# Gated linear attention and a feed-forward layer on one core: columns of the hidden layer renumbered, with another plan of loads and work

## The chip, the cores and the metric

The kernel runs on one core of one Trainium2 chip. The metric is the time of one execution on the device in microseconds (us): 185.11 us, the median of 3 runs (185.07 to 185.2).

## The reference

For each batch b (4) and head h (8), a state of 48 x 48 is carried over 768 steps; its output rows go through a feed-forward layer with 2048 hidden columns:

```python
f = 1.0 / (1.0 + np.exp(-f_logit))
for t in range(S):
    state = f[:, :, t, :, None] * state + np.einsum('bhd,bhe->bhde', k[:, :, t], v[:, :, t])
    y[:, :, t] = np.einsum('bhd,bhde->bhe', q[:, :, t], state)
x = y.transpose(0, 2, 1, 3).reshape(B * S, H * D)      # 3072 x 384
h = x @ w_in                                           # 384 -> 2048
return ((h * (1.0 / (1.0 + np.exp(-h)))) @ w_out)      # 2048 -> 384
```

Inputs and output are float32. The order of the 2048 hidden columns is free as long as w_in's columns and w_out's rows are taken in the same order.

## The kernel before

**Tiles.** The sequence is cut into chunks of 128 steps, 6 for each batch. Two chunks make one of 12 pairs. Pairs 0 to 3 (form T) hold chunks 0 and 1 of one batch, loaded together so that two neighbouring steps lie on one partition (runs of 384 bytes); pairs 4 to 11 (form N) hold the same chunk of two batches (runs of 192 bytes). Within a chunk the recurrence is done as matrices: cumulative sums of log f, their exponentials, q and k scaled by them, scores q k under a triangular mask, and the state carried from chunk to chunk.

**The plan.** Nothing is scheduled by a compiler. The string PLAN lists all work in order; a word is `kind.pair.part:engine:buffers`. Every engine takes its own words in the order in which they stand, and waits in that order (P TensorE, A ScalarE, V VectorE, G GpSimd with its DMA queue, S the DMA queue of SP). The numbers behind the second colon say which buffer of its class a result takes; `pb` are the eight PSUM banks. The kinds:

- `f k q v`: loads from HBM by SP (L225), 384 KB each or in halves. `wi`, `wo`: loads of quarters of w_in and w_out by GpSimd (L204, L207), float32 in HBM, bf16 in SBUF. These weights are loaded once and stay.
- `E`, `L`: exp and ln on ScalarE (L231, L235, L238), together log f. `cs`: cumulative sums on TensorE (L297 to L307). `a`, `ia`, `al`: their exponentials on ScalarE (L309, L311, L253).
- `ki`, `qg`: k and q scaled (L314). `vb`: v cast to bf16. `tq` and `qkc`: both transposed on TensorE (L321) and copied out of PSUM; `qkD` does that by a DMA of SP instead.
- `sc`: scores (L338, L342); `at`: mask (L346); `y`, `yi`: output rows (L260, L354, L358); `yc`: copy (L182 on ScalarE, L184 on VectorE, as all copies); `yT` and `xc`, or `yD`: transposed (L366, or by DMA L370). `d`, `sd`, `su`: the state's update (L272, L375, L379, L385).
- `mi.P.j`: hidden columns 256 j to 256 j + 255 of pair P, 6 matmuls (L246) with 256 columns of x as the moving operand; `mi.P.j.i` is its half for one chunk, 6 matmuls with 128. w_in is the stationary operand, 128 columns side by side for each matmul. `si`: SiLU on ScalarE (L251). `mo.P.i.g`: 4 of the 16 matmuls (L281) that give the output of chunk i of pair P, each for 128 hidden columns and 384 output columns. `oc`: copy out of PSUM, `so`: store (L289 for T, L291 for N).
- `idle.N.n::b`: n matmuls of zeros with N columns, filler for TensorE at the start (L426).

When ScalarE goes over from exponentials to SiLU or back, it loads a table (L477).

w_in is laid out in SBUF as 128 partitions x 3 x 2048 and w_out as 128 x 16 x 384. Hidden column n * 128 + p is column p of the n-th weight block, and row p of w_out's n-th block:

```python
w_in_src = moe_w_in.rearrange("(ko ki) n -> ki ko n", ki=128)
w_out_src = moe_w_out.rearrange("(ko ki) n -> ki ko n", ki=128)
```

A quarter of w_out, as `wo` loads it, therefore reads four separate rows of 1.5 KB for each partition.

Of the kernel before, what the change touches and what calls it, by code (L numbers as in the profile page):

```python
# [49 lines left out]
mi.0.1.0:P:1 vb.2.1:A:5 at.2.0.1:V: mi.0.1.1:P: si.1.2:A: mi.1.0.0:P: si.0.1:A: mi.1.1.1:P: d.2:P:5,7 si.1.0:A: si.1.1:A: y.2:P:0,2 sd.2.0:A:1  # L50
mi.0.5.0:P:1 yc.2.0:A:0 mi.1.4.0:P:3 su.2.0:G:0 mi.1.5.0:P:6 yT.2.0:P:5 mi.1.4.1:P: f.5.0:S:1 xc.2.0:V:2 su.1.1:G:0 mi.0.4.1:P:0 si.1.4:A: yi.2.1:P:
mi.0.4.0:P: yc.2.1:A:2 mi.0.7.1:P:5 wo.0:G: mi.1.5.1:P: yT.2.1:P:3 mi.0.7.0:P: xc.2.1:V: mi.0.5.1:P: sd.2.1:V:1 qg.3.0:G:1 mi.1.7.0:P:2 si.0.5:A:
k.4.0:S:4 mi.2.1:P:3 si.0.7:A: wo.1:G: mi.2.4:P:7 si.1.5:A: vb.3.1:V:6 mi.1.6.0:P:1 si.2.1:A:2 wo.2:G: ki.3.1:V:3 mi.1.7.1:P: ki.3.0:V: mi.2.0:P:5
wo.3:G: si.1.7:A: qg.3.1:V: mi.0.6.0:P:6 si.0.4:A: mi.0.6.1:P: tq.3.0:P:3 si.0.6:A: tq.3.1:P:2 qkc.3.0:V:1 si.2.0:A: mi.2.2:P:0 k.4.1:S: qkc.3.1:A:
mi.2.7:P:6 mi.2.6:P:5 si.2.7:A: cs.4.0:P:3 si.2.4:A: mi.1.6.1:P: vb.3.0:A:1 sc.3.0:P:2,6 si.2.6:A: mi.2.3:P:7 at.3.0.1:V:2 si.2.2:A: mo.1.1.0:P:5
at.3.0.0:V: si.1.6:A: d.3:P:6,0 si.2.3:A: mo.1.0.0:P:2 sd.3.0:V:0 sc.3.1:P:1,7 su.3.0:G:0 mo.1.0.1:P: at.3.1.1:V:3 k.5.1:S:5 al.4.1:A:4 mo.1.1.1:P:
su.2.1:G:0 sd.3.1:V:0 mi.2.5:P:6 at.3.1.0:V: mo.0.0.0:P:7 si.2.5:A: y.3:P:0,1 mo.2.0.0:P:6 mo.2.0.1:P: ia.4.0:A:3 yc.3.0:A:1 mo.0.0.1:P: E.5.0:A:1
f.6.0:S:2 mo.0.1.0:P:0 ia.4.1:A:1 ki.4.0:V:2 yi.3.1:P: mo.1.0.2:P: yc.3.1:A:0 a.4.0:A:2 mo.0.0.2:P: q.4.1:S:4 L.5.0:A:2 mo.1.1.2:P: a.4.1:A:4
mo.0.1.1:P: v.4.0:S:4 yT.3.0:P:1 mo.1.0.3:P: xc.3.0:V:3 q.5.1:S:5 ki.4.1:V:4 cs.5.1:P:4 mo.0.0.3:P: ia.5.1:A:0 v.4.1:S: al.4.0:A:5 oc.1.0:A:0
yT.3.1:P:1 mo.2.0.2:P: al.5.1:A:1 xc.3.1:V: qg.4.1:G: cs.5.0:P:3 q.5.0:S: mo.1.1.3:P: ia.5.0:A:3 E.6.0:A:0 mo.2.0.3:P: qkD.4.1:S:0 a.5.1:A:1  # L60
mi.3.5:P:2 oc.2.0:V:1 a.5.0:A:4 mi.3.4:P:1 qg.5.1:V:0 q.4.0:S: oc.1.1:V:2 mi.3.1:P:4 ki.5.1:V: vb.4.1:G:0 k.5.0:S: mo.0.1.2:P: si.3.5:A:3 vb.4.0:G:2
# [47 lines left out]
def kernel(  # L109
# [398 lines left out]
```

## Time and profile before

| | |
|---|---|
| median of 3 runs | 185.11 us |
| the profiled execution | 184.94 us |
| its span, first to last instruction | 183.2 us |
| TensorE busy | 173.3 us of the span |
| first matmul with w_in | at 24.2 us |
| first matmul with w_out | at 45.7 us |
| w_in issued | at 17.7, 21.6, 25.3 and 26.1 us |
| w_out issued | at 35.9, 37.7, 38.5 and 39.2 us |
| DMA | 31.91 MB in 109478 packets |

The page of the profile gives the busy time of each engine, its share in 40 equal slices, the chain of work that ended last, and the costliest groups of instructions by line. A matmul's time in a group runs from its start until its result is there, so matmuls that follow each other overlap; the rate at which they stream is read from the distance of their starts, or from a run of the same kind in the chain. Weight loads have a row of their own, PEld. DMA-issuing instructions of an engine do not count as busy; the time from issue to landing is told by the DMA view.

### The profile page before, as it was taken

The page shows a single profiled execution, that of the slowest core. Times are in us where ns is not written, and L with a number is a line of the kernel's source. Part 1 is how long each engine was busy: PE and PEld are TensorE (multiplying, and loading weights), DVE is VectorE, ACT ScalarE, POOL GpSimd, SP SyncE. Part 2 cuts the span into 40 slices and gives each one's busy share as a digit, 9 for nine tenths or more (in the row PEclk, how much of TensorE's full clock was granted, in tenths as well). Part 3 has the DMA queues.
Part 4 walks back from the last instruction along what each step waited for, and adds up shares of the span by engine and source line. Part 5 has one row for each costly group of instructions (what it writes and reads, how often), then busy time and mean ns, then how long its engine had stood idle before and what let it go on. Part 6 is the DMA issues. An engine that isn't in the chain of part 4 may idle for free.

```text
span 183.2 us, 4930 instructions
## 1 busy us (share of the span) xinstructions
PE 173.3 (95%) x2014; PEld 126.9 (69%) x2016; DVE 80.8 (44%) x169; ACT 136.1 (74%) x249; POOL 55.5 (30%) x99
## 2 busy tenths in 40 slices
PE   7988898999999999999999999999999999999990
PEld 2356687898666776678788667688766776888650
DVE  6068774052613529184554719340371854500030
ACT  4698997669994895879889995999697662287211
POOL 6043880570404000371055720271310440032010
PEclk9999999999999999999999999999999999999999
DMA  5999999999991997999996999468999997424115
GB/s 136 297 305 300 184 245 254 198 157 203 192 182 36 194 183 127 102 207 188 146 209 139 224 189 198 97 168 165 209 219 143 182 195 143 137 77 177 43 58 160
DMA packets 109478, 31.91 MB, mean 174 GB/s; under 512 B 103504, under 2 KB 109040, under 8 KB 109456
## 3 DMA queue, kind: packets, MB, share of 16 engines
q1 hardware_dynamic: 105136, 26.68, 73.3%
q0 software_dynamic: 4320, 4.92, 14.1%
q8 instruction: 16, 0.26, 0.6%
q14 instruction: 6, 0.05, 0.1%
HBM read 25.17 MB, written 4.72 MB: 163 GB/s over the span
## 4 chain that ended last, share of the span: by engine, by line
PE 76%; DMA 8%; ACT 7%; SPq 2%; DVE 1%; issue 1%; POOL 1%; DVEq 0%
PE pb L281 33%; PE pb L246 29%; DMA w_in_sb<-in_moe_w_in_dram 4%; PE pb L342 3%; DMA f<-in_f_logit_dram 2%; ACT x L309 2%; PE pb L354 2%; PE pb L358 2%; ACT lf L235 1%; DMA out_dram<-ob 1%; SPq L225 1%; PE pb L375 1%; PE pb L304 1%; PE pb L338 1%; POOL st L385 1%
## 5 line engine op out<-in xcount | busy, mean ns | idle before, releaser
L246 PE MATMUL pb<-xT,w_in_sb 128*128 128x256 bf16 (+1 forms) x672 | 69.8, 257 | 1.6 <-DMA w_in_sb<-in_moe_w_in_dram 1.3
L281 PE MATMUL pb<-w_out_sb,hT 128*128 128x384 bf16 x384 | 71.1, 326 | 0.0
L251 ACT ACTIVATE hT<-pb 128x512 bf16<-128x512 f32 x96 | 51.9, 608 | 20.0 <-PE pb L246 19.3
L246 PEld LDWEIGHTS <-w_in_sb 128*128 128x128 bf16 x672 | 57.1, 98 | 9.7 <-DMA w_in_sb<-in_moe_w_in_dram 1.8
L281 PEld LDWEIGHTS <-hT 128*128 128x128 bf16 x384 | 35.0, 97 | 19.6
L385 POOL TENSOR_TENSOR st<-sd,al 48x192 bf16<-48x192 f32 x40 | 20.8, 519 | 56.6 <-PE pb L354 24.1
L346 DVE TENSOR_TENSOR atm<-pb,triu 128x512 bf16<-128x512 f32 x32 | 20.7, 684 | 13.8 <-PE pb L342 12.7
L309 ACT ACTIVATE x<-pb 128x384 f32<-128x384 f32 x48 | 22.2, 512 | 5.9 <-PE pb L307 2.7
L477 ACT ACT_TABLE_LOAD x19 | 24.4, 1283 | 0.3
L184 DVE COPY ob<-pb 128x384 f32<-128x384 f32 x16 | 8.8, 553 | 22.2 <-PE pb L281 19.5
L314 POOL TENSOR_TENSOR qk<-q,x 128x384 bf16<-128x384 f32 x11 | 11.2, 1024 | 21.6 <-ACT x L309 8.4
L314 DVE TENSOR_TENSOR qk<-k,x 128x384 bf16<-128x384 f32 x18 | 10.9, 613 | 12.7 <-ACT x L309 12.7
L182 ACT CAST yb<-pb 128x384 bf16<-128x384 f32 x18 | 9.1, 506 | 7.6 <-PE pb L358 7.4
L379 DVE TENSOR_TENSOR sd<-pb,st 128x384 f32<-128x384 f32 x16 | 8.9, 553 | 11.4 <-PE pb L375 8.6
L291 POOL DMA_DIRECT2D out_dram<-ob x8 | 4.4, 559 | 30.7 <-DVE ob L184 17.0
L346 DVE TENSOR_TENSOR atm<-pb,mask 128x512 bf16<-128x512 f32 x16 | 10.6, 685 | 7.0 <-PE pb L338 6.9
L231 ACT ACTIVATE e<-f 128x768 f32<-128x768 f32 (+1 forms) x13 | 10.6, 812 | 2.8 <-DMA f<-in_f_logit_dram 2.8
L314 DVE TENSOR_TENSOR qk<-q,x 128x384 bf16<-128x384 f32 x13 | 7.2, 561 | 7.7 <-DMA q<-in_q_dram 7.1
L426 PE MATMUL pb<-zero,triu 128*128 128x512 bf16 (+1 forms) x26 | 8.9, 480 | 1.4 <-POOL triu masks.py:66 1.4
L184 DVE COPY xT<-pb 128x384 bf16<-128x384 bf16 x10 | 3.6, 357 | 14.4 <-PE pb L366 14.4
L314 POOL TENSOR_TENSOR qk<-k,x 128x384 bf16<-128x384 f32 x6 | 6.1, 1016 | 8.6 <-ACT x L309 7.5
L182 ACT COPY ob<-pb 128x384 f32<-128x384 f32 x8 | 3.9, 489 | 4.4 <-PE pb L281 4.4
(73 smaller groups left out, 150.3 us busy)
## 6 DMA issues: line engine op xcount, KB each, us to landing
f<-in_f_logit_dram SPq DMA_DIRECT2D x11, 384.0 KB, 5.3
k<-in_k_dram SPq DMA_DIRECT2D x16, 192.0 KB, 3.9
q<-in_q_dram SPq DMA_DIRECT2D x16, 192.0 KB, 3.9
v<-in_v_dram SPq DMA_DIRECT2D x16, 192.0 KB, 3.5
v<-in_v_dram SPq DMA_DIRECT2D x4, 384.0 KB, 7.0
q<-in_q_dram SPq DMA_DIRECT2D x4, 384.0 KB, 5.5
k<-in_k_dram SPq DMA_DIRECT2D x4, 384.0 KB, 5.7
w_in_sb<-in_moe_w_in_dram POOLq DMA_DIRECT2D x4, 384.0 KB, 7.7
```

The source lines that it names most:

```text
L182: nc.scalar.copy(dst, src)
L184: ENG[eng].tensor_copy(dst, src)
L231: return nc.scalar.activation(e, at("f", P)[:, j * w:(j + 1) * w], AF.Exp, scale=-1.0)
L246: nc.tensor.matmul(h[:, i, cols], w_in_sb[:, kk, n * 128:(n + 1) * 128], at("xT", P)[:, kk, cols], start=(kk == 0), stop=(kk == KT - 1))
L251: return nc.scalar.activation(at("hT", P)[:, 2 * j:2 * j + 2, :], at("h", P, j).rearrange("p (n c) -> p n c", n=2), AF.Silu)
L281: nc.tensor.matmul(o, at("hT", P)[:, n, i * C:(i + 1) * C], w_out_sb[:, n, :], start=(n == 0), stop=(n == NT - 1))
L309: nc.scalar.activation(at(kind, P, i).rearrange("p h d -> p (h d)"), at("cs", P, i)[:, 0:HD], AF.Exp, scale=1.0 if kind == "ia" else -1.0)
L314: ENG[eng].tensor_mul(at("qk", P, i)[:, j, :, 0:D], heads("qk"[j], P, i), at("ia" if j else "a", P, i))
L346: ENG[eng].tensor_mul(at("atm", P, i)[:, r], at(f"s{r}", P, i).rearrange("p (n c) -> p n c", c=C), mask[:, None, :].to_broadcast([C, NP, C]))
L379: nc.vector.tensor_add(at("sd", P, i), d_ps, prev_state(P, i))
L385: nc.gpsimd.tensor_mul(at("st", P, i)[lo:lo + D, :, r * D:(r + 1) * D], at("sd", P, i)[lo:lo + D, :, r * D:(r + 1) * D], al_of(P, i)[lo:lo ...
L477: nc.scalar.preload_act_table_set(turns[n])
```

## The change

1. *Hidden columns renumbered.* In a block of 512 hidden columns, partition ki now holds rows 4 ki to 4 ki + 3 of w_out, which lie side by side in HBM: 6 KB in one run for each partition of a quarter. To match, the j-th weight block of w_in takes every fourth column: the stationary operand of `mi` (L246) is now 128 columns with a step of 4 elements. w_in's loads stay as they are.
2. *Another plan.* All words stand in another order, and many copies and products are on another engine: `ki` 15 times on GpSimd and 9 on VectorE (before 6 and 18), `qg` 8 and 16 (11 and 13), `vb` 11 on GpSimd (6), `oc` 15 on ScalarE (8), `xc` 8 on ScalarE (2), `yc` 11 on VectorE (6). SP loads k and q ahead of v at the start and f.3 behind v.2. The words of w_in stand earlier on GpSimd, in the order 2, 1, 0, 3; the two `sc` of a chunk pair stand side by side; pairs 2 and 3 come in later. The fillers are 29 matmuls of 512 columns (before 26) and 4 of 128 (before 2). The transposes of q and k of 4.1 and 5.0 go from DMA to TensorE and that of 6.0 the other way: `tq` stands 11 times (before 10), `qkD` 13 times (before 14); `yT` with `xc` is done for 5.0 in place of 6.0. ScalarE changes its table 17 times within the plan (before 19).
3. *Last results in column halves.* `mo`, `oc` and `so` of pair 11 have a fourth or third number: columns 0 to 191 or 192 to 383 of the output. The 32 matmuls of 384 columns become 64 of 192.

The core of the diff, the start and the end of the plan and the code:

```diff
 PLAN = """
-f.0.0:S:0 f.0.1:S: f.1.0:S:1 v.0.0:S:0 q.0.0:S:0 E.0.0:A:0 E.0.1:A: L.0.0:A:0 k.0.0:S:0 E.1.0:A:1 f.2.0:S:2 L.0.1:A: idle.512.15::7 cs.0.0:P:0
-q.1.0:S:1 cs.0.1:P:1 a.0.0:A:0 L.1.0:A:1 qg.0.0:G:0 a.0.1:A:1 f.3.0:S:3 idle.512.3::7 cs.1.1:P:2 ia.0.0:A:2 ia.0.1:A:3 vb.0.1:G:0 cs.1.0:P:3 ki.0.0:V:
-a.1.0:A:4 k.1.0:S:1 qg.0.1:V:1 ia.1.0:A:0 idle.512.2::7 tq.0.0:P:4 a.1.1:A:2 ki.0.1:V: ia.1.1:A:1 vb.0.0:A:1 idle.512.1::7 tq.0.1:P:5 q.2.0:S:2
-E.2.0:A:0 d.0:P:6,7 qkc.0.1:V:0 L.2.0:A:2 qg.1.1:G:2 qkc.0.0:V: v.1.0:S:1 al.1:A:0 sd.0.0:V:0 idle.512.2::3 cs.2.1:P:0 qg.1.0:V:3 E.3.0:A:1
-sc.0.1:P:3,5 k.2.0:S:2 cs.2.0:P:2 at.0.1.1:V:0 sc.0.0:P:4,6 ia.2.0:A:3 a.2.0:A:2 ki.1.1:V: al.0:A:1 L.3.0:A:0 f.4.0:S:0 ki.1.0:V: su.0.0:G:0
-tq.1.1:P:5 at.0.0.1:V:1 a.2.1:A:4 tq.1.0:P:2 qkc.1.1:A:1 at.0.1.0:V: cs.3.1:P:1 wi.1:G: sd.0.1:V:1 cs.3.0:P:6 qkc.1.0:A: at.0.0.0:V: qg.2.0:G:4
-v.2.0:S:2 al.3:A:2 vb.1.0:A:2 idle.512.3::3 sc.1.0:P:3,5 ia.2.1:A:1 qg.2.1:G:0 y.0:P:7,4 vb.1.1:A:3 at.1.0.0:V:2 k.3.0:S:3 al.2:A:3 a.3.1:A:0
-yi.0.1:P: sc.1.1:P:2,0 ki.2.1:G: at.1.0.1:V: yc.0.0:A:0 ia.3.1:A:2 at.1.1.1:V:3 idle.128.2::3 d.1:P:3,7 yc.0.1:A:1 wi.0:G: ki.2.0:V: tq.2.1:P:5
-ia.3.0:A:4 sd.1.0:A:0 at.1.1.0:V: yT.0.1:P:1 yT.0.0:P:0 a.3.0:A:1 tq.2.0:P:4 su.1.0:G:0 qkc.2.1:V:0 xc.0.0:A:0 y.1:P:3,2 xc.0.1:A: q.3.0:S:3
-qkc.2.0:V: mi.0.2.0:P:6 su.0.1:G:0 yc.1.0:A:2 yi.1.1:P: mi.0.3.1:P:0 E.4.0:A:0 yc.1.1:V:1 sc.2.1:P:5,1 wi.2:G: yT.1.0:P:4 L.4.0:A:1 mi.0.3.0:P:
-...
-si.11.0:A:1 so.7.1:G: mi.11.3:P:6 si.11.1:A: so.4.0:G: mi.11.5:P:5 mi.11.4:P:1 si.11.5:A: mi.11.2:P:3 si.11.4:A: mi.10.3:P:5 si.11.2:A: mi.11.7:P:1
-si.10.3:A: mo.11.1.0:P:3 si.10.6:A: oc.9.0:A:0 mo.10.1.1:P: si.11.3:A: so.9.0:S: mo.11.0.0:P:5 si.11.7:A: mo.10.1.2:P: mo.10.1.3:P: mo.11.0.1:P:
-mo.11.0.2:P: mi.11.6:P:0 mo.11.1.1:P: si.11.6:A: mo.11.1.2:P: mo.11.1.3:P: mo.11.0.3:P: oc.11.1:V:1 mo.10.0.1:P: so.11.1:S: oc.11.0:V:5 mo.10.0.2:P:
-oc.10.1:V:4 so.1.1:S: so.11.0:G: so.10.1:S: mo.10.0.3:P: oc.10.0:A:3 so.10.0:S:
+f.0.0:S:0 f.0.1:S: f.1.0:S:1 k.0.0:S:0 q.0.0:S:0 E.0.0:A:0 E.0.1:A: L.0.1:A:0 f.2.0:S:2 L.0.0:A: idle.512.9::7 cs.0.1:P:0 E.1.0:A:1 cs.0.0:P:1
+q.1.0:S:1 L.1.0:A:1 ia.0.0:A:0 k.1.0:S:1 idle.512.4::7 cs.1.1:P:2 a.0.0:A:1 ki.0.0:V:0 a.0.1:A:2 cs.1.0:P:3 al.1:A:0 ia.0.1:A:3 a.1.1:A:4 v.0.0:S:0
+ki.0.1:G:1 qg.0.1:G: E.2.0:A:0 v.1.0:S:1 a.1.0:A:0 qg.0.0:G: ia.1.0:A:3 idle.512.12::7 tq.0.1:P:4 qg.1.0:V:2 L.2.0:A:2 k.2.0:S:2 wi.2:G: ia.1.1:A:2
+idle.512.1::7 tq.0.0:P:5 qkc.0.1:V:0 qg.1.1:G:3 cs.2.0:P:6 qkc.0.0:V: q.2.0:S:2 a.2.0:A:1 wi.1:G: ki.1.0:V: idle.512.3::3 sc.0.0:P:7,1 sc.0.1:P:3,2
+ki.1.1:G: vb.0.0:A:0 cs.2.1:P:4 at.0.1.0:V:0 vb.0.1:A:1 at.0.0.0:V:1 a.2.1:A:0 wi.0:G: idle.128.1::5 d.0:P:5,3 ia.2.1:A:4 at.0.0.1:V: v.2.0:S:2
+tq.1.0:P:7 al.0:A:1 sd.0.0:A:0 tq.1.1:P:0 at.0.1.1:V: su.0.0:G:0 qkc.1.0:A:1 qkc.1.1:V: idle.128.3::5 y.0:P:1,5 al.2:A:2 ia.2.0:A:3 wi.3:G: yi.0.1:P:
+yc.0.0:A:0 sc.1.1:P:2,7 yc.0.1:A:1 sc.1.0:P:4,0 at.1.1.1:V:2 vb.1.0:G:2 vb.1.1:A:3 yT.0.0:P:6 yT.0.1:P:1 xc.0.0:A:0 at.1.1.0:V: d.1:P:5,7 xc.0.1:A:
+at.1.0.1:V:3 mi.0.5.0:P:6 sd.1.0:A:1 mi.0.5.1:P: at.1.0.0:V: su.1.0:G:0 mi.0.4.0:P:2 mi.0.2.0:P:1 sd.0.1:V:0 y.1:P:5,0 su.0.1:G:0 yi.1.1:P: yc.1.0:A:2
+mi.0.2.1:P: yc.1.1:A:0 mi.0.3.0:P:4 yT.1.0:P:3 mi.0.3.1:P: f.3.0:S:3 xc.1.0:V:1 yT.1.1:P:5 mi.0.4.1:P: xc.1.1:V: mi.1.2.0:P:0 sd.1.1:V:1 si.0.5:A:0
+mi.1.3.0:P:3 mi.1.0.1:P:5 su.1.1:G:0 si.0.4:A: mi.1.5.1:P:7 si.0.2:A: mi.1.3.1:P: mi.1.1.0:P:6 wo.0:G: si.1.3:A:1 mi.1.4.0:P:2 mi.1.2.1:P: wo.1:G:
+mi.1.5.0:P: si.1.2:A: f.4.0:S:0 mi.1.1.1:P: wo.2:G: mi.0.7.1:P:1 si.1.5:A: mi.0.7.0:P: wo.3:G: si.1.1:A: mi.0.6.1:P:3 qg.2.0:V:4 si.0.7:A:
+...
+si.11.5:A: mo.11.0.0.0:P:3 si.11.7:A: mi.10.2:P:6 si.11.2:A: mi.10.5:P:2 si.11.6:A: si.11.3:A: mi.10.4:P:1 si.11.4:A: mo.11.1.0.0:P:7 si.10.2:A:
+mo.11.1.1.0:P: si.10.5:A: mo.11.1.2.0:P: mo.11.1.3.0:P: mo.11.0.1.0:P: oc.11.1.0:V:1 mo.11.1.0.1:P: so.11.1.0:G: mo.11.1.1.1:P: mo.11.0.2.0:P:
+so.8.1:G: mo.10.1.1:P: so.7.1:G: mo.11.0.3.0:P: so.9.0:G: mo.10.0.0:P:5 oc.11.0.0:A:2 si.10.4:A: so.11.0.0:S: mi.10.6:P:4 mo.10.0.1:P: si.10.6:A:
+mo.11.1.2.1:P: mo.10.0.2:P: mo.10.0.3:P: mo.11.1.3.1:P: oc.10.0:A:5 mo.10.1.2:P: oc.11.1.1:V: so.10.0:G: mo.11.0.0.1:P: so.11.1.1:G: mo.10.1.3:P:
+mo.11.0.1.1:P: oc.10.1:A:4 mo.11.0.2.1:P: mo.11.0.3.1:P: so.10.1:S: oc.11.0.1:A: so.11.0.1:S:
 """
...
@@ -158,7 +160,7 @@
     w_in_sb = sb.tile([128, KT, d_ff], BF16, name="w_in_sb")
     w_out_sb = sb.tile([128, NT, d_model], BF16, name="w_out_sb")
     w_in_src = moe_w_in.rearrange("(ko ki) n -> ki ko n", ki=128)
-    w_out_src = moe_w_out.rearrange("(ko ki) n -> ki ko n", ki=128)
+    w_out_src = moe_w_out.rearrange("(m ki j) n -> ki m j n", ki=128, j=4)
     SRC = {"f": f_logit, "k": k, "q": q, "v": v}
 
     plan = []
@@ -192,6 +194,10 @@
     def al_of(P, i):
         return at("al", P)[:, :, i] if PAIRS[P][0] == "T" else at("al", P, i)[:, :, 0]
 
+    def part_of(half):
+        w = d_model // 2
+        return slice(half[0] * w, (half[0] + 1) * w) if half else slice(0, d_model)
+
     def prev_state(P, i):
         b, c = PAIRS[P][1 + i]
         return at("st", *where_u[b, c - 1])
@@ -204,7 +210,7 @@
                 nc.gpsimd.dma_start(out=w_in_sb[:, :, n * w:(n + 1) * w], in_=w_in_src[:, :, n * w:(n + 1) * w])
             else:
                 w = NT // parts
-                nc.gpsimd.dma_start(out=w_out_sb[:, n * w:(n + 1) * w, :], in_=w_out_src[:, n * w:(n + 1) * w, :])
+                nc.gpsimd.dma_start(out=w_out_sb[:, n * w:(n + 1) * w, :].rearrange("p (m j) n -> p m j n", j=4), in_=w_out_src[:, n * w // 4:(n + 1) * w // 4])
             return
         P = rest[0]
         form, *us = PAIRS[P]
@@ -243,7 +249,7 @@
                 n = 2 * j + i
                 cols = slice(rest[2] * C, (rest[2] + 1) * C) if len(rest) > 2 else slice(0, 2 * C)
                 for kk in range(KT):
-                    nc.tensor.matmul(h[:, i, cols], w_in_sb[:, kk, n * 128:(n + 1) * 128], at("xT", P)[:, kk, cols],
+                    nc.tensor.matmul(h[:, i, cols], w_in_sb[:, kk, n // 4 * 512 + n % 4:(n // 4 + 1) * 512:4], at("xT", P)[:, kk, cols],
                                      start=(kk == 0), stop=(kk == KT - 1))
             return
         if kind == "si":
@@ -276,14 +282,16 @@
         b, c = us[i]
         last = c == CHUNKS - 1
         if kind == "mo":
-            o = at("o", P, i)[:, 0:d_model]
+            cols = part_of(rest[3:])
             for n in range(4 * rest[2], 4 * rest[2] + 4):
-                nc.tensor.matmul(o, at("hT", P)[:, n, i * C:(i + 1) * C], w_out_sb[:, n, :], start=(n == 0), stop=(n == NT - 1))
+                nc.tensor.matmul(at("o", P, i)[:, cols], at("hT", P)[:, n, i * C:(i + 1) * C], w_out_sb[:, n, cols], start=(n == 0), stop=(n == NT - 1))
         elif kind == "oc":
-            copy(eng, at("ob", P, i), at("o", P, i)[:, 0:d_model])
+            cols = part_of(rest[2:])
+            copy(eng, at("ob", P, i)[:, cols], at("o", P, i)[:, cols])
         elif kind == "so":
             r0 = b * S + c * C
-            ob, dst = at("ob", P, i), out[r0:r0 + C, :]
+            cols = part_of(rest[2:])
+            ob, dst = at("ob", P, i)[:, cols], out[r0:r0 + C, cols]
             if T:
                 for j in range(2):
                     ENG[eng].dma_start(out=dst.rearrange("(p j) n -> j p n", j=2)[j], in_=ob[j * HC:(j + 1) * HC])
```

## The prediction

> **What bounds the kernel now.** I read the page first (engines, slices, chain), then the chain in order of time, TensorE's waits, the timelines of ScalarE and GpSimd to 40 us, and the DMA landings.
>
> ```profile
> PE 173.3 (95%) x2014; PEld 126.9 (69%) x2016; DVE 80.8 (44%) x169; ACT 136.1 (74%) x249; POOL 55.5 (30%) x99
> ...
> PE   7988898999999999999999999999999999999990
> ...
> PEclk9999999999999999999999999999999999999999
> DMA  5999999999991997999996999468999997424115
> ```
>
> TensorE is full from the eighth slice to the last, at full clock; the DMA engines are full to 55 us (slice 12). The chain, in order of time:
>
> ```profile
> 6.25 0.84 ACT e L231
> ...
> 25.33 8.09 DMA w_in_sb<-in_moe_w_in_dram
> 33.47 1.18 PE pb L246 x18
> 34.65 0.17 PE pb L366 x3
> 34.82 0.67 PE pb L246 x12
> ...
> 63.48 3.27 PE pb L246 x30
> ...
> 174.18 4.56 PE pb L281 x28
> 178.77 0.48 ACT ob L182
> ```
>
> The start is a chain of attention steps and one transfer of w_in; from 33 us on nearly all is matmuls at the streaming rate: 3.27/30 = 109 ns with 256 columns, 4.56/28 = 163 with 384, 0.67/12 = 56 with 128. What TensorE waited for:
>
> ```profile
> PE pb L426 <- POOL triu masks.py:66: 1.4, 1, 1.4
> PE pb L246 <- DMA w_in_sb<-in_moe_w_in_dram: 1.3, 3, 0.7
> PE pb L297 <- ACT lf L235: 0.9, 2, 0.6
> ```
>
> So weights are what it waits for last before it is full. The sum therefore uses one quantity, the **lag**: the clock minus the useful matmul time issued so far (filler matmuls not counted). Per word of the plan I take 0.85 us for the cumulative sums of a T pair, 0.45 for `tq`, 0.35 for `sc` and `d`, 0.42 for a T `y`, 0.17 for `yi` and `yT`, and 0.34 for a half unit of `mi` (6 x 56 ns), all start to start in TensorE's timeline. Ahead of mi.0.7.1, the first that needs w_in's last quarter, these give 19.5 us; it ran when that quarter landed, at 35.9. Lag 16.4. At the end (159.0 us of matmul time, PE done at 178.6) it is 19.6: in 143 us only 3.2 were lost, of which single waits (0.5 at 101.0, 0.3 at 114.7, 0.2 at 110.5) make about 1.1. So time is won by a smaller lag when the weights are in, by less matmul work, or behind the last matmul; nowhere else.
>
> **The change, part by part.**
>
> *Loads and early plan.* When w_in is issued:
>
> ```profile
> 17.68 0.94 POOL L204 DMA_DIRECT2D w_in_sb<-in_moe_w_in_dram  x1
> 18.69 1.95 POOL L314 TENSOR_TENSOR qk<-q,x 128x384 bf16<-128x384 f32 x2
> 20.61 0.98 POOL L314 TENSOR_TENSOR qk<-k,x 128x384 bf16<-128x384 f32 x1
> 21.55 0.79 POOL L204 DMA_DIRECT2D w_in_sb<-in_moe_w_in_dram  x1
> 23.16 2.22 POOL L385 TENSOR_TENSOR st<-sd,al 48x192 bf16<-48x192 f32 x4 [0.83 <-DVE atm L346]
> 25.33 1.55 POOL L204 DMA_DIRECT2D w_in_sb<-in_moe_w_in_dram  x2
> ```
>
> The quarters landed at 24.1, 28.9, 33.4 and 35.9. After the change GpSimd has ki.0.1, qg.0.1 and qg.0.0 ahead of the first. Their start: the first three loads are the same, so E.1.0 begins at 6.25 again; E 0.78 and L 0.73 (start to start) give 7.75; ia.0.0, a.0.0, a.0.1 at 0.39, al.1 at 0.1, ia.0.1 at 0.39 give 9.4; three products at 0.96 give 12.4 (k0 and q0 come a place earlier in SP's queue: k0 where v0 landed, 7.4, and q0 at 8.7 as before). The first quarter (wi.2) is issued at 12.4 instead of 17.7. The next three follow behind qg.1.1, ki.1.1 and su.0.0: issues 14.3, 16.1, 17.9.
>
> Landings: the first quarter needed 6.5 us from issue, so 18.9. Those issued while another was in flight did not start until it had landed, and then came together: w_in's last two 4.5 and 2.5 us apart, w_out's last three 4.3, 2.6 and 2.7 apart. All three stand ready before 18.9, so 23.4 (wi.1), 25.9 (wi.0) and 28.5 (wi.3). SP's loads share the engines as before: in the packet records both queues get the same number of packets while both are full (about 192 each per us at 45 us), and SP's packets are smaller.
>
> Useful time ahead of the first user of each: mi.0.5.0 7.4, mi.0.2.0 8.4 (sums 2.54, `tq` 1.8, `sc` 1.4, `d` 0.7, `y` 0.42, `yi` 0.17, `yT` 0.34, `mi` 1.0), mi.1.0.1 11.7, mi.0.7.1 14.35. Lags: 23.4 - 8.4 = **15.0**, 25.9 - 11.7 = 14.2, 28.5 - 14.35 = 14.15. The attention chain is no later: tq.0.0 about 12.5, scores 14.0, four `at` of VectorE (0.61 each, from 14.7) 17.1, y.0 17.2, yc 17.8, `yT` and xc 19.8, thus mi.0.5.0 at 19.8, lag 12.5. w_out's first quarter is due at 15.0 + 19.6 = 34.6; GpSimd issues it behind su.1.1 at about 26.5, it starts when wi.3 has landed and with 4.3 to 5.6 us is there by 34.1. The lag becomes 15.0 instead of 16.4: **-1.4 us**. Bounds: 13 (quarters together at once) to 18.5 (rival 1).
>
> *Rows of w_out.* 512 runs of 6 KB are read instead of 2048 of 1.5 KB; bytes are equal. Written pieces are 768 B now, 83 ns each in the packet records, 170 us over 16 engines = 10.6. The nearest larger pieces are 1 KB (103 ns, w_in) and 3 KB (138 ns, stores): 512 of 3 KB cost between 4.4 and, at 4 x 83, 10.6 us. Either way it lies beside full matmuls: **0**; without this cover a quarter costs what it lands late, and the first has 0.5 us to spare (34.1 against 34.6). The Trainium skill (DMA: Bandwidth & Descriptors, Specifications) gives 512 B as the least size for line rate; by that 1.5 KB rows lose nothing already and the sum is the same, while the trace's 83 ns for 768 B against 103 ns for 1 KB show that size still matters a little.
>
> *Strided weights.* Every `mi` now loads 128 columns of w_in 4 elements apart. No row shows such a load. Lower end 0; no reason for a gain. Upper end: four times the stretch, four times the time: 224 ns instead of 56, 192 x 168 + 480 x (224 - 109) ns = 87 us. I take 0, since the nearest row, the contiguous load, keeps up with one every 56 ns and 480 of the 672 have 109 ns of streaming to hide in. The Trainium skill (SBUF — State Buffer, note on "SBUF cachelines") speaks of lines of 16 bytes and at least two hits on a line for full rate; 4 bf16 elements are 8 bytes, two hits, so by it the cost is nothing; no row here can show it.
>
> *Matmul work.* One `tq` more (8 x 56 = 0.45; `yT` only moves from pair 6 to pair 5) and pair 11's `mo` as 64 of 192 columns instead of 32 of 384: 64 x 82.5 - 32 x 162.5 = 0.08. **+0.5**.
>
> *Tail.* From the last matmul's end (178.7) to the span's end are 4.45 us: copy 0.48, SP issue 0.34, landing at 181.8, 1.35 to close. The copy of half the columns saves about 0.15 (0.48 with a fixed part; a 4-element one takes 0.19). The transfer is 96 KB instead of 192: pieces of 96 KB landed 2.1 and 2.4 us after issue where this took 2.55. **-0.35**; bounds 0 and -0.6. All other stores are issued earlier; mo.11.0's 12 half-column matmuls (1.0 us) cover oc.10.1 and its store.
>
> *The rest.* `ki`, `vb`, `oc`, `xc`, `yc` change engines: GpSimd gets 9 `ki` more at 1.0 us (30% busy), ScalarE two table loads fewer (1.28 each). Hidden while TensorE is full; without cover a product on GpSimd is 0.4 us later than on VectorE and stands ahead of SP's transposes. Later single waits: 1.1 us now, taken as the same; bounds 0 and 3 (rival 3).
>
> **Sum**: -1.4 + 0.5 - 0.35 = -1.25, from the profiled execution's 184.94 (span 183.2, 1.7 around it): 183.7; its own time is 0.17 below the median of 185.11, so for a median **183.9**.
>
> **Rivals.**
> 1. *The quarters come one by one*, 4.7 us apart, as the second did (24.1 to 28.9): 18.9, 23.6, 28.3, 33.0. mi.0.7.1 then has lag 33.0 - 14.35 = 18.6, since the new order does 5 us less attention work ahead of it: +2.2 + 0.5 - 0.35, **187.4, slower**. It decides from a landing of the last quarter after 30.8 on. For: the second quarter was alone because the third was issued too late. Against: all later ones came in groups. 0.15.
> 2. *Strided loads cost*, at twice the time (112 ns): 56 ns on the 174 half-unit matmuls from mi.0.2.0 on = 9.7, 3 ns on 480 = 1.4: **about 195**. The Trainium skill (Advanced Engine Details and Errata, SBUF Cachelines) tells of a penalty where every access meets another line. 0.1.
> 3. *New single waits eat the gain*: the order of 140 us is new, and one of 1 to 2 us at a transpose or a load brings **185**. For: SP's queue waits in order. Against: TensorE's waits sum to 1.1 now. 0.2.
> 4. *The weights are no bound at all*, lag 13: **182**. 0.05.
>
> Forecast 0.5. A measurement here tells 0.2% (0.37 us) from no change. Faster: forecast 0.47, rival 4, some of 3: 0.57. Same: 0.17, most of 3. Slower: 0.26 (rivals 1, 2, a share of 3). The range runs from 182.5 to rival 1's 187.4; it leaves out rival 2 and the ends.
>
> **What would show it.** First w_in issue near 12.4, landings 18.9, 23.4, 25.9, 28.5; a wait of about 2 us of L246 near 21; lag 15.0 at mi.0.7.1 (29.4 us); w_in's weight loads at 98 ns and `mi` at 109; end of PE to span end 4.1. Wrong: `mi` above 112 ns, a wait at 30 us, waits of over 1 us after 40.

## The result: slower, and the profile after

| | before | after |
|---|---|---|
| median of 4 runs | 185.16 us | 192.75 us |
| ratio to before, 95% interval | | 1.041 [1.0369, 1.0452] |
| profiled execution, its span | 184.94, 183.2 us | 192.34, 190.5 us |
| first matmul with w_in | 24.2 us | 25.7 us |
| lag at 35 us | 16.1 | 22.8 |
| TensorE done, to the span's end | 178.7, 4.45 us | 187.4, 3.08 us |

Medians are over all executions of a kernel; ratios leave out those that took over 1.5% more than its fastest.

The change costs 7.6 us where 1.2 of gain were forecast. The lag is counted as in the prediction. The page after, engines and slices:

```profile
PE 173.2 (91%) x2060; PEld 136.8 (72%) x2061; DVE 76.5 (40%) x155; ACT 134.1 (70%) x253; POOL 66.2 (35%) x115
...
PE   7889219999999999999979999998899998999993
...
PEclk9999855999999999999999999999999999999998
DMA  6999999999989900999359398795999599520133
```

TensorE's busy time is what it was. Two things are new: the hole in the fifth and sixth slice (19 to 28.6 us), and a granted clock that falls to half there and stays low for a slice after it. The last row, DMA, shows no such hole there: the transfers went on while TensorE stood.

What TensorE waited for, line by line: total, times, longest.

```profile
PE pb L252 <- DMA w_in_sb<-in_moe_w_in_dram: 6.5, 2, 4.1
PE pb L434 <- POOL triu masks.py:66: 1.4, 1, 1.4
PE pb L374 <- ACT yb L184: 1.2, 1, 1.2
PE pb L252 <- ACT xT L184: 1.1, 1, 1.1
PE pb L252 <- DVE sd L387: 1.1, 1, 1.1
```

Before, the matmuls with w_in waited 1.3 us for it, in three pieces; now 6.5 in two. TensorE's timeline (start, length, and in brackets the idle time before) shows where:

```profile
21.08 0.52 PE L278 MATMUL pb<-vb,qk 64*128 64x96 bf16 x16
25.74 0.27 PE L252 MATMUL pb<-xT,w_in_sb 128*128 128x128 bf16 x1 [4.14 <-DMA w_in_sb<-in_moe_w_in_dram]
28.33 2.64 PE L252 MATMUL pb<-xT,w_in_sb 128*128 128x128 bf16 x23 [2.32 <-DMA w_in_sb<-in_moe_w_in_dram]
```

One matmul, and then another wait. GpSimd issued the quarters of w_in as forecast (those of w_out, the last row, only at 36.21 instead of 26.5, since the state's update ahead of them waited too):

```profile
12.64 0.95 POOL L210 DMA_DIRECT2D w_in_sb<-in_moe_w_in_dram  x1
...
14.55 0.79 POOL L210 DMA_DIRECT2D w_in_sb<-in_moe_w_in_dram  x1
...
16.31 0.79 POOL L210 DMA_DIRECT2D w_in_sb<-in_moe_w_in_dram  x1
...
18.18 0.79 POOL L210 DMA_DIRECT2D w_in_sb<-in_moe_w_in_dram  x1
...
36.21 2.21 POOL L213 DMA_DIRECT2D w_out_sb<-in_moe_w_out_dram  x4
```

By the semaphore events of the trace they landed at 20.64 (wi.2), 23.04 (wi.1), 25.61 (wi.0) and 28.28 (wi.3). mi.0.5.0 uses hidden columns 1280 to 1535, which lie in wi.2 alone, and that was there at 20.64, before the matmuls ahead were done (21.6). Its first matmul ran 0.1 us behind the *third* landing and its second 0.05 us behind the *fourth*. The program's own waits say the same: the first weight load of mi.0.5.0 waits for wi.2, wi.1 and wi.0, the second for wi.3. In the kernel before, the first waits for the one quarter that it reads. So these are no waits of the chip: they stand in the program, which takes a slice of w_in with a step of 4 for something that any of the four loads may write. How it comes to that, and why the fourth load is waited for one matmul later, is not shown.

The clock, from the table of stretches (length, PE busy, PEld, DVE, ACT, POOL, then PEclk, DMA share, GB/s):

```profile
20.00:22.00 2.00, 1.13 (x22) 0.71 (x22) 2.00 (x4) 2.00 (x6) 0.00 (x0) 1.00 1.20 206
22.00:24.00 2.00, 0.00 (x0) 0.00 (x0) 0.04 (x1) 0.31 (x1) 1.46 (x3) 0.56 1.21 208
...
28.00:30.00 2.00, 1.67 (x16) 1.67 (x17) 0.00 (x0) 0.00 (x0) 0.00 (x0) 0.50 0.89 185
30.00:32.00 2.00, 2.00 (x47) 1.74 (x45) 0.00 (x0) 0.24 (x1) 0.00 (x0) 0.50 0.94 233
32.00:34.00 2.00, 2.00 (x35) 2.00 (x33) 0.53 (x2) 1.22 (x3) 0.00 (x0) 0.88 0.94 181
```

The clock fell at 22.26 us and came back at 32.49, 4.2 us after work had begun again; in these 4.2 us the matmuls did half their work, so about 2 us went there. The books close: lag at 35 us +6.66, time that TensorE lost between matmuls after that +1.55 (4.99 against 3.44), matmul work +0.65, tail -1.37, sum +7.49, where the spans differ by 7.35.

And the end, from the timeline of all engines:

```profile
187.03 1.12 SPq L299 DMA_DIRECT2D out_dram<-ob  x2
187.47 0.32 ACT L184 COPY ob<-pb 128x192 f32<-128x192 f32 x1 [0.47 <-PE pb L287]
```

### The profile page after: what moved, and what is told of

It is laid out like the page before. It is cut to its first block, busy times and chain, and to the rows that moved or that the text cites. A ratio compares the mean times of both kernels' runs of the same rounds, so it can differ in the third digit from the quotient of the medians.

```text
span 190.5 us, 5036 instructions
## 1 busy us (share of the span) xinstructions
PE 173.2 (91%) x2060; PEld 136.8 (72%) x2061; DVE 76.5 (40%) x155; ACT 134.1 (70%) x253; POOL 66.2 (35%) x115
## 4 chain that ended last, share of the span: by engine, by line
PE 52%; DMA 15%; POOL 12%; ACT 11%; issue 4%; SPq 3%; DVE 2%; POOLq 0%; ACTq 0%
PE pb L252 23%; PE pb L287 20%; POOL qk L322 6%; DMA w_in_sb<-in_moe_w_in_dram 5%; ACT x L317 4%; POOL st L393 3%; DMA out_dram<-ob 3%; ACT hT L257 3%; DMA q<-in_q_dram 2%; DMA f<-in_f_logit_dram 2%; DMA v<-in_v_dram 2%; SPq L231 2%; PE pb L362 1%; ACT e L237 1%; POOL w_in_sb L210 1%
## 5 line engine op out<-in xcount | busy, mean ns | idle before, releaser
L252 PEld LDWEIGHTS <-w_in_sb 128*128 128x128 bf16 x672 | 64.4, 115 | 11.7 <-issue 7.0
L287 PE MATMUL pb<-w_out_sb,hT 128*128 128x384 bf16 (+1 forms) x416 | 71.4, 314 | 0.7 <-ACT hT L257 0.5
L317 ACT ACTIVATE x<-pb 128x384 f32<-128x384 f32 x48 | 22.1, 507 | 3.2 <-PE pb L305 1.3
L322 POOL TENSOR_TENSOR qk<-k,x 128x384 bf16<-128x384 f32 x15 | 15.2, 1015 | 22.6 <-ACT x L317 10.1
L184 ACT COPY ob<-pb 128x384 f32<-128x384 f32 (+1 forms) x15 | 7.1, 470 | 12.9 <-PE pb L287 11.1
L387 DVE TENSOR_TENSOR sd<-pb,st 128x384 f32<-128x384 f32 x16 | 8.7, 552 | 14.4 <-POOL st L393 9.0
L186 DVE COPY ob<-pb 128x384 f32<-128x384 f32 (+1 forms) x11 | 5.6, 517 | 20.7 <-ACT hT L257 11.8
L322 DVE TENSOR_TENSOR qk<-q,x 128x384 bf16<-128x384 f32 x16 | 10.3, 660 | 8.8 <-ACT x L317 7.9
L184 ACT CAST yb<-pb 128x384 bf16<-128x384 f32 x13 | 6.2, 482 | 10.7 <-PE pb L266 9.5
L299 POOL DMA_DIRECT2D out_dram<-ob x9 | 5.1, 564 | 22.8 <-DVE ob L186 17.0
L186 POOL CAST vb<-v 128x384 bf16<-128x384 f32 x11 | 6.1, 564 | 17.7 <-DMA v<-in_v_dram 17.5
L186 DVE CAST yb<-pb 128x384 bf16<-128x384 f32 x11 | 6.0, 555 | 13.0 <-PE pb L366 7.7
L322 POOL TENSOR_TENSOR qk<-q,x 128x384 bf16<-128x384 f32 x8 | 8.3, 1041 | 1.2 <-ACT x L317 1.0
```

The lines of the kernel that those rows point to most:

```text
L184: nc.scalar.copy(dst, src)
L186: ENG[eng].tensor_copy(dst, src)
L252: nc.tensor.matmul(h[:, i, cols], w_in_sb[:, kk, n // 4 * 512 + n % 4:(n // 4 + 1) * 512:4], at("xT", P)[:, kk, cols], start=(kk == 0), st ...
L287: nc.tensor.matmul(at("o", P, i)[:, cols], at("hT", P)[:, n, i * C:(i + 1) * C], w_out_sb[:, n, cols], start=(n == 0), stop=(n == NT - 1))
L317: nc.scalar.activation(at(kind, P, i).rearrange("p h d -> p (h d)"), at("cs", P, i)[:, 0:HD], AF.Exp, scale=1.0 if kind == "ia" else -1.0)
L322: ENG[eng].tensor_mul(at("qk", P, i)[:, j, :, 0:D], heads("qk"[j], P, i), at("ia" if j else "a", P, i))
```

## The experiments

**Theories.** A: the slice with a step makes the program wait for all quarters; w_in in four SBUF tiles, one per quarter, must mend it, since then no load can be taken for another. B: the strided weight load itself is slow. C: the new order of loads and work is at fault. The label of each run stands over its expectation. All ratios are to the kernel before, run beside each kernel.

### The plan without the renumbering

```diff
-w_in_sb[:, kk, n // 4 * 512 + n % 4:(n // 4 + 1) * 512:4]
+w_in_sb[:, kk, n * 128:(n + 1) * 128]
-w_out_src = moe_w_out.rearrange("(m ki j) n -> ki m j n", ki=128, j=4)
+w_out_src = moe_w_out.rearrange("(ko ki) n -> ki ko n", ki=128)
```

> The changed kernel with the hidden columns in their old order (w_in blocks of 128 neighbouring columns, w_out in rows of 1.5 KB); plan and column halves stay. Theory A (every fourth column makes the first matmuls with w_in wait for all four quarters, and the stall lets the clock fall to half): the first w_in matmul starts at 20.7 us when its own quarter lands instead of 25.7 and 28.3, no slice at half clock, lag near 15 where it was 23: 184.5 us. Theory B (loading every fourth column is slow in itself): also near 185, so A and B are not told apart here. Theory C (the new plan itself loses the time, by its later waits): above 189.

186.35 us, ratio 1.0013 [0.9979, 1.0047]. The 7.6 us are gone, so C is not the cause; the plan by itself wins nothing either, where 184.5 was expected. The first matmul with w_in came at 22.4 (the profiled execution took 187.96 us). New is a wait of 0.74 and one of 0.56 us for w_out (from start to start of the matmuls around them), whose quarters (again of 1.5 KB rows) landed at 36.71, 39.44, 42.10 and 44.83: 2.7 us apart. One thing was expected to go and did not: in this execution, too, the clock was at half, from 21.66 to 25.07, though no matmul waited for w_in. The first matmuls with w_in ran about 106 ns apart instead of 56:

```profile
20.98 0.72 PE L374 MATMUL pb<-ident,yb 128*128 128x128 bf16 x6 [1.23 <-ACT yb L184]
...
22.39 2.74 PE L252 MATMUL pb<-xT,w_in_sb 128*128 128x128 bf16 x24
```

Of the eight executions in the ratio four have a mean granted clock of 0.991, which is one such stretch (3.4 us at half in 184), and a median of 186.6 us; four have 1.000 and 185.6. So the new plan can lose time to the clock with no false wait at all, here about 1 us.

### The renumbering in the plan of before

The edit above, the other way round, in the kernel before.

> The kernel before with the renumbering alone; plan as before, no column halves. Theory A: the first w_in matmul moves from 24.2 to 28.9 us (it now also waits for the second quarter) and the next but few to 35.9 (third and fourth quarter), at 10 us of useful matmul time instead of 19.5; TensorE's clock falls to half on the way: about 195 us. Theory B: the first w_in matmul stays at 24.2, the rate of the matmuls falls. Theory C: no change, 185.1.

204.98 us, ratio 1.1023 [1.0975, 1.1072]: slower by 10 us than expected. The page's slices and TensorE's wait for w_in:

```profile
PE   7678723209999999999999999999999999999991
...
PEclk9999975556999999999999999999999999999999
```

```profile
PE pb L246 <- DMA w_in_sb<-in_moe_w_in_dram: 17.1, 3, 6.2
```

GpSimd's timeline has the reason:

```profile
21.73 0.79 POOL L204 DMA_DIRECT2D w_in_sb<-in_moe_w_in_dram  x1
...
31.36 0.79 POOL L204 DMA_DIRECT2D w_in_sb<-in_moe_w_in_dram  x1 [5.77 <-PE pb L246]
...
38.92 0.76 POOL L204 DMA_DIRECT2D w_in_sb<-in_moe_w_in_dram  x1 [6.76 <-PE pb L246]
```

The false dependency works both ways. In this plan some `mi` stand ahead of the last two loads, so the loads wait until those matmuls have read "their" columns, and the next matmuls wait for the loads: load and work take turns, three waits of 5 to 6 us. The changed kernel has all four loads ahead of the first `mi` and was spared this half.

### w_in in four tiles

```diff
-w_in_sb = sb.tile([128, KT, d_ff], BF16, name="w_in_sb")
+w_in_sb = [sb.tile([128, KT, d_ff // 4], BF16, name=f"w_in_sb{m}") for m in range(4)]
...
-w_in_sb[:, kk, n // 4 * 512 + n % 4:(n // 4 + 1) * 512:4]
+w_in_sb[n // 4][:, kk, n % 4:512:4]
```

> The changed kernel with w_in in four SBUF tiles, one for each quarter, in place of one; every fourth column is still what is loaded, plan, w_out's rows of 6 KB and column halves stay. Theory A: as the plan without renumbering, the first w_in matmul at 20.7 us, 184.5 us or a little less. Theory B: 192 us as the changed kernel, since the loads are the same. Theory C: above 189.

185.28 us, ratio 0.9987 [0.9952, 1.0022]. The same strided loads and the same plan are 7.5 us faster than the changed kernel: A holds. TensorE's timeline:

```profile
22.11 1.21 PE L252 MATMUL pb<-xT,w_in_sb 128*128 128x128 bf16 x18
24.38 0.53 PE L252 MATMUL pb<-xT,w_in_sb 128*128 128x128 bf16 x6 [1.06 <-DMA w_in_sb<-in_moe_w_in_dram]
```

18 matmuls with the first quarter (three half units of wi.2) follow on the work ahead of them without a wait, and the next wait 1.06 us for the second, as the plan means it. The clock stays at 1.00 in this execution; in five of the ten it is 0.988 to 0.991, and here their median is the same as that of the others (185.3).

### Four tiles in the plan of before

The two edits together in the kernel before.

> The kernel before with the renumbering and with w_in in four tiles; plan as before. Theory A: strided loads and rows of 6 KB by themselves, with no wait added: 185.1 us within 0.4, w_in matmuls at 109 ns with 256 columns and 56 with 128, w_out's quarters a little closer together (2.2 us apart instead of 2.6 to 2.7). Theory B: over 187.

185.78 us, ratio 1.0004 [0.9979, 1.0029]. So the strided load costs nothing that can be measured, and B falls. It does take longer; the rows of before, then of this kernel (ns: least, median, most):

```profile
L246 PEld LDWEIGHTS <-w_in_sb x672: 95/98/100, 24.2 to 173.8; 128*128 128x128 bf16 x168
```

```profile
L246 PEld LDWEIGHTS <-w_in_sb x672: 111/113/133, 24.8 to 174.2; 128*128 128x128 bf16 x168
```

15 ns more each, and still the matmuls start 109 and 56 ns apart. The rows of 6 KB help the loads and not the time: the last three quarters of w_out landed 1.75 and 2.0 us apart (45.51, 47.26, 49.29) where before it was 2.6 and 2.7, beside matmuls that did not wait for them.

### How much of it is the clock

20 (first run: 30) matmuls of no use ahead of mi.0.5.0 in the changed kernel; nothing reads their result.

```diff
-at.1.0.1:V:3 mi.0.5.0:P:6
+at.1.0.1:V:3 idle.512.20::6 mi.0.5.0:P:6
```

> The changed kernel with 30 more filler matmuls of 512 columns (216 ns each at full clock, 6.5 us) ahead of its first matmul with w_in, so that TensorE is busy while it would wait for the quarters. If the half clock from 22.3 to 32.5 us comes from the wait and costs something of its own: no slice at half clock, the w_in matmuls of 128 columns at 56 ns from 28.3 us on instead of 106, 2.0 us less, 190.5 us. If the clock costs nothing: 192.7, or more where filler delays work.

> The changed kernel, with 20 matmuls of no use (their result is never read) ahead of the first mi, some 5.8 us of TensorE's time, which should end about when the last quarter of w_in lands (28.3). The waits for the quarters stay. If the lower clock after the idle time costs about 2 us of the 7.6, the w_in matmuls of 128 columns run at 56 ns from the start and the time is 190.5 to 190.8. If the lower clock costs nothing (other work would have been late anyway), it stays at 192.7.

30 fillers: 192.07 us, ratio 1.0285 [1.0124, 1.0447]; the interval is wide, since the kernel before lay between 184.5 and 187.8 us beside it. In the profiled execution (193.51 us) the clock had fallen at 22.5, so they ran on to 30.7, 1.6 us after the last landing there (29.1):

```profile
30.68 1.50 PE L252 MATMUL pb<-xT,w_in_sb 128*128 128x128 bf16 x24
```

That is 2.35 us later than the run of `mi` began in the changed kernel (28.33); yet at 35 us the lag was 23.3, only 0.5 more than there, because `mi` then ran at 56 ns at once. By this the low clock is worth 1.9 us.

20 fillers: 191.76 us, ratio 1.0289 [1.0235, 1.0342], between the two values expected. In the profiled execution they ran at full clock and were done too soon:

```profile
21.57 4.48 PE L434 MATMUL pb<-zero,triu 128*128 128x512 bf16 x19
25.89 0.22 PE L252 MATMUL pb<-xT,w_in_sb 128*128 128x128 bf16 x1
28.53 1.83 PE L252 MATMUL pb<-xT,w_in_sb 128*128 128x128 bf16 x23 [2.42 <-DMA w_in_sb<-in_moe_w_in_dram]
```

The 2.42 us of idle time were enough here: the clock was at half from 29.49 to 32.9. One of its four executions had a granted clock of 1.000, and took 190.36 us, near the 190.5 to 190.8 expected of a full clock; the others, at 0.989 to 0.991, took 191.14 to 192.54. That agrees with some 2 us, but it is one execution: the 2 us for the clock are worked out from the traces and not measured by themselves.

### The end in halves, and an earlier store

In the plan of before: the very last result (`mo`, `oc`, `so` of 10.0) in two column halves; and, apart from that, so.1.1 moved from SP's last stores to a place ahead of so.9.0.

```diff
-mo.10.0.3:P: oc.10.0:A:3 so.10.0:S:
+mo.10.0.3.0:P: oc.10.0.0:A:3 so.10.0.0:G: mo.10.0.0.1:P: mo.10.0.1.1:P: mo.10.0.2.1:P: mo.10.0.3.1:P: oc.10.0.1:A: so.10.0.1:S:
```

> The kernel before with the last result alone (chunk 0 of pair 10) in column halves: the first half is copied and stored while the second half's four matmul groups run; nothing else changes, no renumbering. From the last matmul's end to the span's end it has 4.4 us, the changed kernel 3.1. If halves are what shortens the end: 0.15 less in the copy, 0.3 to 0.9 less in the landing, 184.2 to 184.7 where before is 185.1. If it is the fewer stores in flight (five of 192 KB were issued in the last 2 us before, two after): a gain of 0.2 at most.

> The kernel before with one store moved: the result of pair 1's chunk 1 (192 KB, ready since about 75 us) leaves on SP at about 170 us instead of 177, so that one store less stands in the queues at the end. If stores in flight lengthen the last landing (2.55 us from issue, 1.6 in the changed kernel): 0.3 to 0.5 less. If not: the same within 0.2%.

Halves: 185.21 us, ratio 0.9991 [0.9963, 1.0019]. From TensorE's end to the span's end are 3.68 us instead of 4.45, but the second half paid for it:

```profile
178.27 1.48 PE L285 MATMUL pb<-w_out_sb,hT 128*128 128x192 bf16 x16 [0.41 <-ACT ob L182]
```

Both halves lie in one PSUM bank, and the second half's first matmul waited until the first half had been copied out. In the changed kernel matmuls of other results come between the two halves of a result, and that wait shrinks to one of 0.2 us:

```profile
PE pb L287 <- DVE ob L186: 0.2, 1, 0.2
```

The earlier store: 184.72 us, ratio 0.9976 [0.9941, 1.0012], which is not told from no change. Its profiled execution took 441 us and says nothing of the others, so what the stores in flight cost stays open.

### Taking out what waits remained

With four tiles there were still single waits (counted from start to start of the matmuls around them; the view of waits, which goes by the modelled end of the matmul ahead, has some 0.2 us less) of 1.32 us at 90.0 (xc.5.0 on ScalarE, behind a table load), 0.92 at 125.9 (`sd` on VectorE behind su.7.1, which stood on GpSimd behind a product and two stores) and 0.70 at 151.6 (a SiLU on ScalarE behind copies that waited for stores). The four tiles, and:

```diff
-xc.5.0:A:
+xc.5.0:V:
...
+su.7.1:G:0
 ki.9.1:G:4
...
 so.2.1:G:
+so.6.1:G:
...
-su.7.1:G:0
...
 so.0.0:S:
+so.1.0:S:
...
-so.6.1:G:
...
-so.1.0:S:
```

> The changed kernel with w_in in four tiles, and three places of its plan mended that TensorE waits for: the copy of pair 5's transposed rows on VectorE instead of ScalarE, where it stands behind a table load (wait of 1.33 us at 90); pair 7's state update ahead of a product and a store on GpSimd (0.92 at 126); two old stores earlier, so that two result copies on ScalarE do not wait for their buffers (0.9 at 151). Theory A (the plan won 0.4 us at the start and 1.4 at the end and gave it back by these waits): 3.1 less than with four tiles alone, 182.2, at worst 183.5 where a next wait takes the place. If the waits only show what is late anyway: 185.

184.05 us, ratio 0.9912 [0.9881, 0.9943]: faster than both kernels, though by 1.2 us against four tiles alone and not by the 3.1 expected. In the profiled execution, at 182.3 us the fastest of the twelve, all three waits are gone; one of 1.16 us at 136.0 was new. From its waits:

```profile
PE pb L383 <- POOL vb L186: 1.0, 1, 1.0
```

`vb`, the cast of v, was done by GpSimd behind three products. Three more kernels went after it: its cast on VectorE; that with its load earlier; the earlier load alone.

```diff
-vb.9.0:G:4
+vb.9.0:V:4
...
 v.9.1:S:3
+v.9.0:S:
...
 q.10.1:S:
...
 k.11.0:S:5
...
-v.9.0:S:
```

> The kernel of e8_three_waits_taken_out, with vb.9.0 copied by VectorE instead of GpSimd. Its profile showed one wait of over a microsecond left on TensorE: 1.16 us at 136.0, for vb.9.0, which stood behind products on GpSimd. If that wait was the whole of it, the time falls by about 1.0 us against e8 (184.05 median; ratio about 0.986 to before, span near 179.5). If another unit's operand is late next, TensorE waits for that instead and the time is e8's (ratio about 0.991).

> The kernel of e9_fourth_wait_taken_out (vb.9.0 on VectorE), with the load v.9.0 right behind v.9.1 in SP's queue, so ahead of q.10.1 and k.11.0. In e9 TensorE's wait stayed at 1.1 us because VectorE itself sat idle until v.9.0 had landed, 5.1 us after its issue at 133.60. Two loads earlier are about 1.75 us earlier. If the load is what is late, the wait of L383 is gone and the time is 1.0 us below e8 and e9 alike in the profile (lag at the end lower by 1.0), near 183.2 for a median. If another operand is next, the wait moves and the time is that of e9 (184.6) or e8 (184.05).

> The kernel of e8_three_waits_taken_out (vb.9.0 on GpSimd), with the load v.9.0 moved as in e11. There GpSimd was busy from 132.2 to 136.7 without a gap, then cast vb.9.0, whose load had landed at 135.46. If GpSimd's order sets that wait, the earlier load changes nothing: a wait of 1.0 to 1.2 us of L383 for vb remains, time as e8 (184.05). If the load alone sets it, the wait is gone and the time is as in e11.

The cast on VectorE: 184.61 us, ratio 0.9944 [0.9911, 0.9976]; TensorE still waits 1.1 us, since VectorE itself waited for the load:

```profile
138.71 0.73 DVE L186 CAST vb<-v 128x384 bf16<-128x384 f32 x1 [2.96 <-DMA v<-in_v_dram]
```

The load alone: 183.9, ratio 0.9936 [0.9906, 0.9967]; GpSimd still comes to it last, behind a product:

```profile
137.15 0.99 POOL L322 TENSOR_TENSOR qk<-q,x 128x384 bf16<-128x384 f32 x1
138.09 0.50 POOL L186 CAST vb<-v 128x384 bf16<-128x384 f32 x1
```

Both together: 184.07, ratio 0.9895 [0.9855, 0.9934]; the wait for `vb` is gone, and another took its place, 1.4 us at 144.0 from start to start, for a transpose of SP:

```profile
PE pb L252 <- DMA xT<-yb: 1.2, 1, 1.2
```

Load and engine were both late, each hiding the other, and behind them a third. The intervals of these four overlap, so which of them is best stays open; that they are faster than before is shown.

## Why the prediction was wrong, point by point

1. **The step that failed** is "Useful time ahead of the first user of each", by which each `mi` waits for its own quarter: mi.0.5.0 for the first, mi.0.2.0 for the second, and so "23.4 - 8.4 = 15.0". The trace of the changed kernel shows mi.0.5.0 behind the third and fourth landing, and the lag at 35 us is 22.8. Four tiles alone bring it back to 16.1 and the time from 192.75 to 185.28. The part on strided weights asked only how long such a load takes; what else the step of 4 does, namely which transfers the program then waits for, was not asked. No rival had it, and the time lies above the range of 182.5 to 187.4.
2. **The half clock** adds to it: of the +6.66 in lag some 2 us, as worked out above. The clock fell at 22.26, only 0.7 us into the false wait, and without the renumbering it fell too (21.66); what the false wait added is that TensorE stood until 28.33 and the clock stayed low until 32.49.
3. **Issues right, landings nearly.** Issues 12.64, 14.55, 16.31, 18.18 against 12.4, 14.3, 16.1, 17.9. Landings 20.64, 23.04, 25.61, 28.28 against 18.9, 23.4, 25.9, 28.5: the first needed 8.0 us and not 6.5, the others came 2.4 to 2.7 apart and not 4.5 first. Rival 1 (4.7 apart) is out. The attention chain came later than forecast: the work ahead of mi.0.5.0 was done at 21.6 (with four tiles 22.1) and not at 19.8, with a wait of 1.2 us for `yb` in it. With four tiles the second quarter came later still, so this did not set the lag there. There w_out was issued from 29.5 on instead of 26.5 and its first quarter landed at 34.27, against 34.1.
4. **The plan's gain of 1.4 us did not come** even without the false wait: with four tiles the lag is 16.1 where the kernel before has 16.1. There the second quarter landed at 24.34 instead of 23.4, which is 0.9 of the miss. In the executions of this plan that were profiled the first issue lay between 12.6 and 14.4 us and the second landing between 22.9 and 24.4; the lag at 35 us was 14.8 in the one of the three removed waits, where the second quarter landed at 22.98, and 16.1 to 16.4 in the others without the false wait. So 15.0 is its good case.
5. **Strided weights: 0 was right** (four tiles in the plan of before: 1.0004), though the loads are not "at 98 ns" but at 113. The Trainium skill (SBUF — State Buffer, note on "SBUF cachelines") asks for two hits on a line of 16 bytes for full rate, which a step of 8 bytes has: the rate of the matmuls, unchanged at 56 and 109 ns, agrees, the 15 ns on each load show that it isn't quite free by itself. Rival 2 is out.
6. **Rows of 6 KB: 0 was right** for the time, with cover. The Trainium skill (DMA: Bandwidth & Descriptors, Specifications) gives 512 B as the least transfer for line rate; here w_out's quarters landed 1.75 and 2.0 us apart instead of 2.6 and 2.7 when the written pieces grew, so size still counted above it, beside SP's loads on the same engines. The pieces of 3 KB took 253 ns each on average, 8.1 us over 16 engines in all, within the 4.4 to 10.6 of the prediction. In the new plan without them w_out was waited for (0.74 and 0.56 us).
7. **Matmul work** +0.65 against +0.5: right. **Tail** -1.37 against -0.35 and beyond the bound of -0.6: the copy is 0.32 instead of 0.48, but most of it is the last transfer (1.61 us from issue to landing instead of 2.55) and what follows it (1.09 instead of 1.35), which the rows of other pieces of 96 KB did not show. Halves alone, in the plan of before, took 0.77 off; where the rest comes from is not shown.
8. **Rival 3 was true as well.** Single waits after 40 us sum to 4.5 us against 0.8 by the same count (those over 0.25 us): 0.38, 1.33, 1.28, 0.51, 0.70 and 0.34. With four tiles they, and the rest of the time lost after 35 us, cost 1.0 us more than before and eat the gain of the tail: 0.9987. Three of them taken out gave 0.9912.

## What to carry to other kernels

When a change makes an operand strided, compare what the program waits for before and after, not only what the operation costs: look for the first user of a tile that is loaded in parts, and whether its waits name the part that it reads or all of them. A tile for each part that is loaded by itself takes the question away. And when waits are taken out one by one, an operand can be late for two reasons at once, its load and its engine; only both edits together show what lies behind them.

## What the runs showed of the hardware

The low clock came in whole stretches of 3.41 us: 22.49 to 25.90 and 29.49 to 32.90 in the two kernels with fillers, 21.66 to 25.07 without the renumbering, 21.24 to 24.65 in the kernel with load and cast both moved, and 22.26 to 32.49 (three times 3.41) in the changed kernel. With 20 fillers it fell a microsecond after work had begun again (29.49, work from 28.53), so it followed the time before and not the moment. The 3.41 us ahead of that fall held 2.42 us of idle time; those ahead of 21.66 and 21.24 held one wait of 1.2 us, for `yb`. With four tiles the same wait stands in the trace (1.24 us) and the clock did not fall, so how much idle time is enough is not settled here. The Trainium skill (TensorE: Matmul & The Clock Gate, Part 1: The HAM clock gate) has windows of about 3.4 us, idle for half the clock and busy for the full one: the lengths agree, but none of these three stretches ahead of a fall was idle throughout.
